# The beginning of a fused attention and two-layer MLP kernel: query transposes ahead of exponentials, row sums by ScalarE, three input weights prepared by GpSimd

## The chip, the cores and the metric

The kernel runs on 1 core of one Trainium2 chip. The metric is the device time of one execution in microseconds; three executions of the kernel before gave 1700.34, 1700.97 and 1705.41 us, a median of 1700.97 us.

## What is computed

Attention over keys and values that are averaged in groups of 8 rows, and then two MLPs of 4608 tokens, 512 to 2048 to 512, the first with a squared relu, the second with a leaky relu:

```python
k_p = k.reshape(B, H, Sp, 8, D).mean(axis=3)         # B = H = 8, D = 64, S = 576, Sp = 72
v_p = v.reshape(B, H, Sp, 8, D).mean(axis=3)
scores = scale * np.matmul(q, k_p.transpose(0, 1, 3, 2))
attn = np.exp(scores - np.max(scores, axis=-1, keepdims=True))
attn = attn / (np.sum(attn, axis=-1, keepdims=True) + 1e-09)
x = np.matmul(attn, v_p)                              # then to [4608, 512]
h = np.maximum(x @ w_in, 0.0);  x = h * h @ w_out     # moe_w_in, moe_w_out
h = x @ w2_in;  out = np.maximum(0.01 * h, h) @ w2_out
```

The weights arrive as 64-bit floats, and the kernel reads them as pairs of 32-bit words.

## The kernel before

**Tiling.** Tokens go in blocks of 512 (four tiles of 128). Matrix products are made in a split form: each operand is a high and a low part, and three products are added. One unit of the first product is 12 matmuls of 128x512 (`first`, L883). The kernel starts with the attention of block 0 alone (`start`), then makes 32 units of first products (`first_products`) of blocks 0 and 1, into which the attention of block 1 and the preparation of the weights are woven. After that everything is interleaved, and TensorE has work throughout.

**Order.** The program is recorded by hand: each engine runs its instructions in the order in which the code writes them. `START` is a list of words that `start()` (L749 on) works off: `K` and `Q` load keys and queries, `V` values and `i` a weight; `k0` pools, masks and transposes the keys of batch 0; `q` transposes a query tile and copies it out of PSUM with ScalarE (L567); `s` makes scores (L598), their negated maxima (VectorE, L610) and the exponentials (ScalarE, L619); `n` normalizes a tile (L630 to L640: row sums, reciprocal, product, and two copies of a remainder into one of two `prem` slots); `P` transposes the normalized tile and its remainder with TensorE (L661, L667) and copies the high part out with ScalarE (L671, L673); `r` makes the low part with VectorE (L680) and so gives the PSUM banks back; `v0` pools the values with TensorE (L392) and sums halves with VectorE (L402); `m0` splits the pooled values (L526 to L541); `w0` places them with ScalarE (L524); `x1` pools the keys of batch 1 with TensorE (L392). Then `values` (L712 to L715) makes the attention's output, and the first unit follows.

**Weights.** A weight of layer 1 is one load of 1 MB and seven steps (`weight_steps`): `a` scales the top words (ScalarE, L231), `b` shifts and merges their bits (VectorE, L235, L238), `c` cuts out the exponent and scales the low words by it (L249, L252), `d` adds (L293), `D` rounds to the high part (ScalarE, L298), `e` subtracts for the low part (VectorE, L302). All are 128x1024. Input weight n (0 to 7) is first used by units 2n and 2n+1. Weight 0 is made in `START`, the others by `conversion(u)` beside unit u; `val`, the work buffer, has 2 copies.

**Buffers and queues.** `bank()` hands out 4 PSUM banks in turn; `acc_bank` names four others. Loads are issued by SP in program order; stores of the first product's output (`mid`, L1098) are issued by GpSimd, which before the change does nothing else in the program but three memsets. The rows of `r`, from which they store, have 3 copies.

Of the kernel before, what the change touches and what calls it, by code (L numbers as in the profile page):

```python
# [16 lines left out]
P = 128  # L17
# [26 lines left out]
def attention_relu2_leaky_kernel(  # L44
# [27 lines left out]


# [3 lines left out]
        "K0 Q0 i0 Q1 Q2 Q3 V0 i1 K1 i2 Q4 Q5 i3 "  # L77
        "q0 k0 a0 s0 q1 b0 s1 q2 c0 n0 s2 q3 n1 s3 P0 d0 n2 r0 P1 n3 r1 a1 v0 P2 r2 m0 P3 r3 w0 e0 x1"
# [168 lines left out]
    def low_term(val, top, low):  # L247
# [4 lines left out]
        nc.vector.scalar_tensor_tensor(  # L252
            out=f32(low),
            in0=low,
            scalar=2.0**-52,
            in1=f32(top),
            op0=ALU.mult,
            op1=ALU.mult,
        )
# [13 lines left out]
    def weight_steps(w, kind, i):  # L273


        st = {}

# [10 lines left out]
        def term():  # L288
            low_term(st["val"], st["top"], st["low"])
# [14 lines left out]
        return load_words, lambda: exponent(st["top"]), bits, term, high, low, high_copy  # L304
# [77 lines left out]
    first_tiles, first_s, early = range(T // P), [], range(2 * T // P)  # L382
# [93 lines left out]
    def v_pool_pe(b):  # L476
# [3 lines left out]
        ps, last = acc_bank(2), acc_bank(3)  # L480
# [4 lines left out]
        halves_sum(vps[b], ps, 0, NP)  # L485
        halves_sum(vrps[b][:RROWS], last, 0, 2)
# [88 lines left out]
    def score_products(i):  # L575
# [12 lines left out]
        for hf in range(2):  # L588
            if i in first_tiles:
                ps = acc_bank((2 * i + hf) % KC)  # L590
            else:
                ps = acc_bank(KC - 1) if i in early and hf == 0 else bank()
# [145 lines left out]
    def start():  # L738

        t0, rest = 0, {}  # L740
        for word in START:
# [18 lines left out]
            elif x in "abcde":  # L760
                w1.do("dD" if x == "d" else x, n)
# [9 lines left out]
            elif x == "v":  # L771
                v_pool_pe(n)
                drop("v", n, NP)
                drop("rem", n, 2)
            elif x == "m":
# [282 lines left out]
    def conversion(u):  # L1058
        if u in begins:
# [595 lines left out]
```

## Time and profile before

| | |
|---|---|
| three runs | 1700.34, 1700.97, 1705.41 us |
| the profiled execution | 1704.66 us, of it the span 1702.9 us |
| busy: TensorE matmul, weight load | 1663.1 us (98%), 1500.0 us (88%) |
| busy: VectorE, ScalarE, GpSimd | 1156.0 us (68%), 703.9 us (41%), 19.6 us (1%) |
| first matmul of the first unit | 44.75 us from the span's start |

The span is the time between the first and the last recorded instruction; 1.8 us of the execution lie around it. In the rows below, PE is TensorE, DVE VectorE, ACT ScalarE, POOL GpSimd and SP the engine that issues loads. L12 is line 12 of the kernel before; in the kernel after, the functions that are named here stand 10 to 29 lines lower.

### The profile page before, as it was taken

How to read it: one execution, taken by the hardware profiler on the slowest of the kernel's cores; microseconds unless marked ns; L12 is line 12 of the kernel's file. 1: busy time of each engine (PE TensorE's matmuls, PEld its weight loads, DVE VectorE, ACT ScalarE, POOL GpSimd, SP SyncE). 2: the span in 40 equal slices, each digit the busy share in tenths (PEclk: the TensorE clock that was granted, in tenths of full speed). 3: DMA queues.
4: the chain of work that ended last, by engine and by line, in shares of the span. 5: the costliest groups of instructions: out<-in, count | busy, mean ns of one | idle time of the engine just before them, and what ended most of it. 6: DMA issues, size and time to landing. Idle time of an engine off the chain costs nothing. (4 is left out here: it accounts for less than half of the span.)

```text
span 1702.9 us, 25369 instructions
## 1 busy us (share of the span) xinstructions
PE 1663.1 (98%) x9608; PEld 1500.0 (88%) x9608; DVE 1156.0 (68%) x2028; ACT 703.9 (41%) x1551; POOL 19.6 (1%) x39
## 2 busy tenths in 40 slices
PE   6999999999999999999999999999999999999998
PEld 5778888888888888888888899999999999999998
DVE  7978886666666667575534677756767866666665
ACT  4545343343443443433433444434444633333332
POOL 0012000000000000000000000000000000000000
PEclk9999999999999999999999999999999999999999
DMA  8924542323233232332001255355437755454443
GB/s 229 342 88 156 173 152 94 89 89 96 88 98 98 86 97 74 96 110 73 30 25 56 86 172 177 118 179 174 170 126 257 259 164 164 150 158 155 155 149 106
DMA packets 197211, 228.24 MB, mean 134 GB/s; under 512 B 49120, under 2 KB 157920, under 8 KB 197088
## 3 DMA queue, kind: packets, MB, share of 16 engines
q1 hardware_dynamic: 193952, 217.70, 39.8%
q0 software_dynamic: 2560, 8.39, 1.3%
q8 instruction: 75, 1.23, 0.3%
q10 hardware_dynamic: 576, 0.52, 0.1%
q14 instruction: 48, 0.39, 0.1%
HBM read 140.58 MB, written 85.98 MB: 133 GB/s over the span
## 5 line engine op out<-in xcount | busy, mean ns | idle before, releaser
L883 PE MATMUL ps<-xh,wi 128*128 128x512 f32 x896 | 296.6, 393 | 0.0
L921 PE MATMUL acc<-gh,wo 128*128 128x512 f32 x1080 | 276.6, 394 | 0.7 <-ACT xl L893 0.7
L921 PEld LDWEIGHTS acc<-gh,wo 128*128 128x128 f32 x1080 | 200.7, 189 | 41.7 <-ACT xl L893 1.2
L883 PEld LDWEIGHTS ps<-xh,wi 128*128 128x128 f32 x896 | 168.2, 188 | 34.6 <-issue 0.2
L883 PE MATMUL ps<-xl,wi 128*128 128x512 f32 x448 | 174.4, 389 | 0.0
L900 DVE CAST gh<-r 128x512 fp32r<-128x512 f32 x112 | 47.6, 425 | 175.0 <-ACT r L896 174.6
L893 ACT ACTIVATE r<-ps 128x512 f32<-128x512 f32 x112 | 67.7, 605 | 207.8 <-PE ps L883 203.6
L921 PE MATMUL acc<-gl,wo 128*128 128x512 f32 x540 | 149.5, 390 | 0.0
L921 PEld LDWEIGHTS acc<-gl,wo 128*128 128x128 f32 x540 | 101.8, 189 | 21.6
L619 ACT ACTIVATE s<-ps,m 128x72 f32<-128x72 f32 x240 | 72.1, 330 | 93.4 <-DVE m L610 93.4
L883 PEld LDWEIGHTS ps<-xl,wi 128*128 128x128 f32 x448 | 84.2, 188 | 16.5
L1537 PE MATMUL acc<-wi,hh 128*128 128x256 f32 x512 | 94.0, 283 | 1.1 <-ACT r L1353 1.1
L1537 PE MATMUL acc<-wo,hh 128*128 128x256 f32 x512 | 93.8, 283 | 0.0
L1537 PE MATMUL ps<-wo,hh 128*128 128x256 f32 x496 | 90.9, 283 | 0.0
L1537 PE MATMUL ps<-wi,hh 128*128 128x256 f32 x496 | 90.9, 283 | 0.0
L1337 PE MATMUL acc<-fh,wi 128*128 128x384 f32 x408 | 88.4, 339 | 1.3 <-DVE gh L1350 0.3
L1337 PE MATMUL ps<-fh,wo 128*128 128x384 f32 x408 | 87.7, 337 | 0.0
L901 DVE TENSOR_TENSOR gl<-r,gh 128x512 fp32r<-128x512 f32 x112 | 77.6, 693 | 7.5
L1537 PEld LDWEIGHTS acc<-wi,hh 128*128 128x128 f32 x512 | 79.9, 192 | 1.3 <-ACT r L1353 1.3
L1537 PEld LDWEIGHTS acc<-wo,hh 128*128 128x128 f32 x512 | 79.9, 192 | 0.0
L1353 ACT ACTIVATE gh<-gh 128x384 f32<-128x384 f32 x48 | 25.3, 526 | 131.1 <-DVE gh L1350 131.1
L1537 PEld LDWEIGHTS ps<-wo,hh 128*128 128x128 f32 x496 | 77.4, 192 | 0.0
(278 smaller groups left out, 3560.9 us busy)
## 6 DMA issues: line engine op xcount, KB each, us to landing
hf<-r SPq DMA_DIRECT2D x96, 192.0 KB
xl<-hf SPq DMA_DIRECT2D x24, 640.0 KB
hr<-hf SPq DMA_DIRECT2D x24, 640.0 KB
xh<-hf SPq DMA_DIRECT2D x23, 640.0 KB
hf<-gl SPq DMA_DIRECT2D x48, 192.0 KB
hf<-gh SPq DMA_DIRECT2D x48, 192.0 KB
hf<-st SPq DMA_DIRECT2D x48, 192.0 KB
wi<-in_moe_w_in SPq DMA_DIRECT2D x8, 1024.0 KB
```

Source lines behind the costliest of these rows:

```text
L619: nc.scalar.activation(out=s[:, g, :], in_=ps[:, h * SP : (h + 1) * SP], func=AF.Exp, bias=m[:, g : g + 1], accum_out=None if i in early e ...
L883: nc.tensor.matmul(ps, lhsT=w[:, kc], rhs=x[kc], start=(kc == 0 and n == 0), stop=(kc == KC - 1 and n == 2),)
L893: nc.scalar.activation(out=r, in_=ps, func=AF.Relu)
L900: nc.vector.tensor_copy(gh, r)
L901: nc.vector.tensor_tensor(out=gl, in0=r, in1=f32(gh), op=ALU.subtract)
L921: nc.tensor.matmul(acc[m], lhsT=w[:, m * P : (m + 1) * P], rhs=x, start=(c == 0 and n == 0), stop=(c == FC - 1 and n == 2),)
L1337: nc.tensor.matmul(at, lhsT=w[:, FORMS[j], kc], rhs=x[j][:, kc], start=m == 0 and j not in (4, 6), stop=m == 5, skip_group_check=True,)
L1353: nc.scalar.activation(out=out_, in_=x, func=AF.Lrelu)
L1537: nc.tensor.matmul(at[:, s * TR : (s + 1) * TR], lhsT=x[:, a, s * P : (s + 1) * P], rhs=w[:, b], start=p == 0 and s == 0 and m == 0, stop= ...
```

## The change

It reorders `START`, lets GpSimd do steps `a`, half of `c`, `d` and `e` of input weights 0, 1 and 3, lets ScalarE's exponentials add up the rows of the first eight tiles, and moves steps of weights 1 to 3 between the beginning and the units.

```diff
+    BY_GPSIMD = (0, 1, 3)
     START = (
-        "K0 Q0 i0 Q1 Q2 Q3 V0 i1 K1 i2 Q4 Q5 i3 "
-        "q0 k0 a0 s0 q1 b0 s1 q2 c0 n0 s2 q3 n1 s3 P0 d0 n2 r0 P1 n3 r1 a1 v0 P2 r2 m0 P3 r3 w0 e0 x1"
+        "K0 Q0 Q1 Q2 i0 Q3 V0 i1 K1 i2 Q4 Q5 i3 "
+        "q0 k0 q1 s0 q2 s1 n0 q3 s2 a0 b0 c0 d0 n1 P0 s3 v0 r0 n2 P1 D0 a1 e0 "
+        "n3 u0 P2 m0 b1 c1 d1 r1 P3 w0 r2 x1 r3"
     ).split()
...
+    def exponent(top, engine=None):
+        if engine is None:
+            nc.scalar.activation(out=f32(top), in_=f32(top), func=AF.Copy, scale=2.0**-112)
+        else:
+            engine.tensor_scalar(out=f32(top), in0=f32(top), scalar1=2.0**-112, scalar2=None, op0=ALU.mult)
...
+    def low_term(val, top, low, engine=None):
+        engine = engine or nc.vector
         nc.vector.tensor_scalar(
             out=top, in0=val, scalar1=0xFF800000, scalar2=None, op0=ALU.bitwise_and
         )
+        if engine is nc.vector:
...
+        else:
+            engine.tensor_scalar(out=f32(low), in0=low, scalar1=2.0**-52, scalar2=None, op0=ALU.mult)
+            engine.tensor_tensor(out=f32(low), in0=f32(low), in1=f32(top), op=ALU.mult)
...
+        by = nc.gpsimd if kind == 0 and i in BY_GPSIMD else None
+        engine = by or nc.vector
...
-            nc.vector.tensor_tensor(out=w, in0=w, in1=f32(st["low"]), op=ALU.add)
+            engine.tensor_tensor(out=w, in0=w, in1=f32(st["low"]), op=ALU.add)
...
-            nc.vector.tensor_tensor(out=t[:, 1], in0=st["w"], in1=f32(t[:, 0]), op=ALU.subtract)
+            engine.tensor_tensor(out=t[:, 1], in0=st["w"], in1=f32(t[:, 0]), op=ALU.subtract)
...
-    first_tiles, first_s, early = range(T // P), [], range(2 * T // P)
+    first_tiles, first_s, early = range(T // P), [], range(0)
...
-        ps, last = acc_bank(2), acc_bank(3)
+        ps, last = bank(), bank()
         for cc in range(NP):
             halves(ps, cc, raws[("v", b, cc)][0], P)
         for c in range(2):
             halves(last, c, raws[("rem", b, c)][0], RROWS)
-        halves_sum(vps[b], ps, 0, NP)
-        halves_sum(vrps[b][:RROWS], last, 0, 2)
+        def rest():
+            halves_sum(vps[b], ps, 0, NP)
+            halves_sum(vrps[b][:RROWS], last, 0, 2)
+        return rest
...
     def conversion(u):
-        if u in begins:
+        if u == 0:
+            w1.do("De", 1)
+            w1.do("abcd", 2)
+        elif u == 1:
+            w1.do("D", 2)
+            w1.do("ab", 3)
+        elif u == 2:
+            w1.do("e", 2)
+            w1.do("c", 3)
+        elif u == 3:
+            w1.do("d", 3)
+        elif u == 4:
+            w1.do("De", 3)
+            w1.do("a", 4)
+        elif u in begins:
```

With `early` empty, the exponentials of tiles 0 to 7 get an accumulator output and the row sums of L630 are gone. The word `v` now only makes the products; `u` makes the two sums; `d` no longer includes `D`.

**TensorE, from tile 3's scores to the values**, where `acc_382<-gh` (before) and `acc_385<-gh` (after) begin `x1`. Before, from the second `P`:

```order
L661 MATMUL ps<-cst,wo_160 128x128 x4
L667 MATMUL ps<-cst,prem_82 96x128 x2
L392 MATMUL acc_314<-wo_99,cst 128x128 x12
L392 MATMUL acc_314<-wo_104,cst 128x128 x4
L392 MATMUL acc_315<-wo_104,cst 96x128 x8
L661 MATMUL ps<-cst,wo_160 128x128 x4
L667 MATMUL ps<-cst,prem_81 96x128 x2
L661 MATMUL ps<-cst,wo_250 128x128 x4
L667 MATMUL ps<-cst,prem_82 96x128 x2
L392 MATMUL acc_382<-gh,cst 128x128 x4
```

After, from the pooling of the values:

```order
L402 MATMUL ps<-wo_99,cst 128x128 x12
L402 MATMUL ps<-wo_104,cst 128x128 x4
L402 MATMUL ps<-wo_104,cst 96x128 x8
L675 MATMUL ps<-cst,wo_165 128x128 x4
L681 MATMUL ps<-cst,prem_82 96x128 x2
L675 MATMUL ps<-cst,wo_165 128x128 x4
L681 MATMUL ps<-cst,prem_81 96x128 x2
L675 MATMUL ps<-cst,wo_264 128x128 x4
L681 MATMUL ps<-cst,prem_82 96x128 x2
L402 MATMUL acc_385<-gh,cst 128x128 x4
```

The pooling of the values moved from behind `P1` to ahead of it and out of the named banks into two of the four that `P` uses in turn; `P1`, `P2`, `P3` and `x1` now follow each other.

**VectorE at the same place.** Before, from the copies of tile 3's remainder:

```order
L640 COPY prem_82<-wo_250 128x96 x2
L680 TENSOR_TENSOR ptl<-ps,pth 128x4x128
L680 TENSOR_TENSOR ptr<-ps,ptr 32x2x128
L402 TENSOR_REDUCE vp<-acc_314 128x256
L402 TENSOR_REDUCE vr<-acc_315 96x128
```

After, from the sums of the pooled values, which follow the same copies:

```order
L412 TENSOR_REDUCE vr<-ps 96x128
L540 TENSOR_SCALAR vh<-vp 128x256
L550 SCALAR_TENSOR_TENSOR vp<-vp,vh 128x256
L540 TENSOR_SCALAR rh<-vr 96x128
L550 SCALAR_TENSOR_TENSOR vr<-vr,rh 96x128
L540 TENSOR_SCALAR vr<-vr,cst 96x128
L555 SCALAR_TENSOR_TENSOR vr<-rh,cst,vr 96x128
L239 TENSOR_SCALAR val<-wi_112 128x1024
L242 SCALAR_TENSOR_TENSOR val<-wi_112,val 128x1024
L253 TENSOR_SCALAR wi_112<-val 128x1024
L694 TENSOR_TENSOR ptl<-ps,pth 128x4x128
```

`r1` (the last row) stood right behind the copies; now the value sums, `m0` and the bit steps of weight 1 (`wi_112`) stand ahead of it.

**GpSimd**, which had no instruction between the memset of `v_rem` and the first store of `mid`. After:

```order
L235 TENSOR_SCALAR wi_97<-wi_97 128x1024
L266 TENSOR_SCALAR wi_97<-wi_97 128x1024
L267 TENSOR_TENSOR wi_97<-wi_97 128x1024
L303 TENSOR_TENSOR val<-val,wi_97 128x1024
L235 TENSOR_SCALAR wi_112<-wi_112 128x1024
L312 TENSOR_TENSOR wi_245<-val,wi_245 128x1024
L266 TENSOR_SCALAR wi_112<-wi_112 128x1024
L267 TENSOR_TENSOR wi_112<-wi_112 128x1024
L303 TENSOR_TENSOR val<-val,wi_112 128x1024
L312 TENSOR_TENSOR wi_363<-val,wi_363 128x1024
L1127 DMA mid<-r 128x512
```

Weight 0 (`wi_97`, `wi_245`) and weight 1 (`wi_112`, `wi_363`) take five instructions each, and `a` of weight 1 stands ahead of `e` of weight 0.

## Rows read from the trace of the kernel before

**Rows 1.** The page's first part: busy us, share of the span, instructions.

```profile
PE 1663.1 (98%) x9608; PEld 1500.0 (88%) x9608; DVE 1156.0 (68%) x2028; ACT 703.9 (41%) x1551; POOL 19.6 (1%) x39
```

**Rows 2.** Windows: length, busy us of each engine, granted clock, DMA share, GB/s.

```profile
0.00:44.70 44.70, 28.33 (x181) 25.37 (x182) 32.57 (x64) 21.84 (x59) 0.73 (x5) 0.96 0.84 233
44.70:110.00 65.30, 57.89 (x305) 46.48 (x305) 55.72 (x96) 33.36 (x81) 6.53 (x11) 0.97 0.70 252
25.00:30.00 5.00, 4.66 (x26) 4.62 (x27) 3.90 (x10) 3.65 (x12) 0.00 (x0) 0.66 1.04 272
```

**Rows 3.** Timeline of PE, 29 to 45: start, us, engine, line, operation.

```profile
29.40 5.49 PE L392 MATMUL acc<-wo,cst 128*128 128x128 f32 x48
...
35.56 0.62 PE L661 MATMUL ps<-cst,wo 128*128 128x128 f32 x4
...
36.24 1.06 PE L392 MATMUL acc<-gh,cst 128*128 128x128 f32 x8
...
40.92 0.50 PE L712 MATMUL ps<-pth,v_hi 128*128 128x512 f32 x1
...
44.75 0.40 PE L883 MATMUL acc<-xh,wi 128*128 128x512 f32 x1
```

**Rows 4.** Timeline of DVE, 34 to 51.

```profile
34.28 0.41 DVE L640 COPY prem<-wo 128x96 f32<-128x96 f32 x2
34.72 0.69 DVE L680 TENSOR_TENSOR ptl<-ps,pth 128x512 fp32r<-128x512 f32 x1
...
35.90 0.69 DVE L402 TENSOR_REDUCE vp<-acc 128x256 f32<-128x512 f32 x1
...
36.95 0.69 DVE L680 TENSOR_TENSOR ptl<-ps,pth 128x512 fp32r<-128x512 f32 x1
...
38.12 0.29 DVE L526 TENSOR_SCALAR vh<-vp 128x256 fp32r<-128x256 f32 x1
...
40.06 0.69 DVE L680 TENSOR_TENSOR ptl<-ps,pth 128x512 fp32r<-128x512 f32 x1
...
47.77 0.68 DVE L235 TENSOR_SCALAR val<-wi 128x1024 uint32<-128x1024 uint32 x1
...
50.48 1.23 DVE L252 SCALAR_TENSOR_TENSOR wi<-wi 128x1024 f32<-128x1024 uint32 x1
```

**Rows 5.** Timeline of SP's issues and of ACT: two landings.

```profile
28.11 5.67 SPq L197 DMA_DIRECT2D raw<-in_q  x3
...
31.17 1.16 ACT L231 ACTIVATE wi<-wi 128x1024 f32<-128x1024 f32 x1 [0.20 <-DMA wi<-in_moe_w_in]
```

**Rows 6.** Waits of PE, 44.7 to 110: us in total, times, longest.

```profile
PE acc L883 <- DVE wi L302: 2.2, 4, 1.0
```

**Rows 7.** Timelines of POOL's issues and of DVE beside them, 54 to 88.

```profile
54.85 0.54 POOL L1098 DMA_DIRECT2D mid<-r  x1 [3.23 <-ACT r L893]
...
73.73 0.76 POOL L1098 DMA_DIRECT2D mid<-r  x1 [9.53 <-ACT r L893]
...
86.68 0.77 POOL L1098 DMA_DIRECT2D mid<-r  x1 [11.19 <-ACT r L893]
...
54.74 1.22 DVE L302 TENSOR_TENSOR wi<-val,wi 128x1024 fp32r<-128x1024 f32 x1
...
73.69 0.68 DVE L235 TENSOR_SCALAR val<-wi 128x1024 uint32<-128x1024 uint32 x1
...
86.66 0.68 DVE L235 TENSOR_SCALAR val<-wi 128x1024 uint32<-128x1024 uint32 x1
```

**Rows 8.** Timeline of POOL, its first microseconds.

```profile
0.73 0.52 POOL L1612 MEMSET v_rem<- 128x512 f32 x1 [0.29 <-POOLq L1634]
```

**Rows 9.** Line L630, duration in ns min/median/max, first and last start.

```profile
L630 DVE TENSOR_REDUCE l<-wo x4: 742/746/752, 20.2 to 32.2; 128x8 f32<-128x576 f32 x4
```

**Rows 10.** Line L619, the same columns.

```profile
L619 ACT ACTIVATION_READ_ACCUMULATOR s<-ps,m x224: 191/213/243, 182.3 to 868.9; 128x1 f32 x112
```

More of the change, by code (lines that the diff above doesn't have):

```diff
@@ L245, in first_bits @@
         )
-    def low_term(val, top, low):
+    def low_term(val, top, low, engine=None):
+        engine = engine or nc.vector
         nc.vector.tensor_scalar(
@@ L251, in low_term @@
         )
[L252 to L259, printed above, removed]
+        if engine is nc.vector:
+            engine.scalar_tensor_tensor(
+                out=f32(low),
+                in0=low,
+                scalar=2.0**-52,
+                in1=f32(top),
+                op0=ALU.mult,
+                op1=ALU.mult,
+            )
+        else:
+            engine.tensor_scalar(out=f32(low), in0=low, scalar1=2.0**-52, scalar2=None, op0=ALU.mult)
+            engine.tensor_tensor(out=f32(low), in0=f32(low), in1=f32(top), op=ALU.mult)
     def place(kind, i, t):
@@ L288, in term @@
         def term():
-            low_term(st["val"], st["top"], st["low"])
+            low_term(st["val"], st["top"], st["low"], by)
         def high():
             w = st["w"] = f32(st["val"])
-            nc.vector.tensor_tensor(out=w, in0=w, in1=f32(st["low"]), op=ALU.add)
+            engine.tensor_tensor(out=w, in0=w, in1=f32(st["low"]), op=ALU.add)
             t = st["parts"] = sb([P, 2, 1024], F32R, weight_tag(kind, i))
@@ L301, in low @@
             t = st["parts"]
-            nc.vector.tensor_tensor(out=t[:, 1], in0=st["w"], in1=f32(t[:, 0]), op=ALU.subtract)
-        return load_words, lambda: exponent(st["top"]), bits, term, high, low, high_copy
+            engine.tensor_tensor(out=t[:, 1], in0=st["w"], in1=f32(t[:, 0]), op=ALU.subtract)
+        return load_words, lambda: exponent(st["top"], by), bits, term, high, low, high_copy
     class Weights:
@@ L591, in score_products @@
             else:
-                ps = acc_bank(KC - 1) if i in early and hf == 0 else bank()
+                ps = acc_bank(KC - 1) if i < 2 * T // P and hf == 0 else bank()
             for b, _, r0, n in reversed(parts_of(i)):
@@ L759, in start @@
                 w1.load(n)
-            elif x in "abcde":
-                w1.do("dD" if x == "d" else x, n)
+            elif x in "abcdeD":
+                w1.do(x, n)
             elif x == "k":
@@ L771, in start @@
             elif x == "v":
-                v_pool_pe(n)
+                sums = v_pool_pe(n)
                 drop("v", n, NP)
                 drop("rem", n, 2)
+            elif x == "u":
+                sums()
             elif x == "m":
@@ L1062, in conversion @@
                 w1.do("a", n + 1)
-            w1.do("bcd" if n == 1 else "cdD", n)
+            if n > 3:
+                w1.do("cdD", n)
         elif u - 1 in begins:
             n = begins[u - 1]
-            if n == 1:
-                w1.do("D", n)
             if n < LAST and n + 1 != LATE:
                 w1.do("b", n + 1)
-            if n != LATE - 1:
+            if n not in (3, LATE - 1):
                 w1.do("e", n)
```

2 lines of the change are left out of this document (removed).

## The prediction

> **What bounds the kernel now.** I read the page's first part, then windows of the first 110 us, then the timelines of TensorE and VectorE there. TensorE's matmuls fill 98% of the span [rows 1], so a gain or a loss must come from the places where it has nothing to do. Two of them lie in the changed part: up to the first unit it is busy 28.33 of 44.70 us, and in the next 65.30 us it is busy 57.89 us [rows 2], which leaves 7.4 us. VectorE is busy 32.57 and 55.72 us there. The forecast is therefore about two things: when the first unit starts (44.75, [rows 3]), and what the 7.4 us become.
>
> What ends the beginning is read from the timeline of TensorE [rows 3]. From 29.40 it works nearly without a gap: the pooling of the values (5.49 us), then `P2`, `P3` (from 35.56), `x1` (from 36.24), the values (from 40.92) and the first unit. From `x1` to the values are 40.92 - 36.24 = 4.68 us, and from the values to the unit 3.83 us. What VectorE does meanwhile (`r1`, sums, `r2`, `m0`, `r3`, [rows 4]) runs beside `x1`. The two landings that count are fixed by the loads: SP's issue at 28.11 had waited for a load of the values, the last of the remainder, and weight 1 lands at about 31.1, where ScalarE waited for it [rows 5].
>
> **Part 1: the order of the beginning, with GpSimd's work at no cost.** The loads of tiles 1 and 2 go ahead of weight 0. Its landing moves back by two loads of 256 KB, about 2 us at the 233 GB/s of this stretch [rows 2]; nobody waits for it, since its bits now come behind the maxima of tile 2. Nothing is moved ahead of the remainder of the values or of weight 1 that was not ahead of them before, so both land as before.
>
> Now the pooling of the values stands ahead of `P1`, and TensorE can't pass 28.11. The last of its six groups of matmuls takes 5.49 / 6 = 0.9 us, so `P1` starts at 29.0 and, by the 0.68 us from `P3` to `x1` [rows 3], ends at 29.7. VectorE's copies of tile 3's remainder need the slot that `P1` reads: they start at 29.7. From there VectorE decides, by [rows 4]: copies 0.44 (34.28 to 34.72), sums 1.05 (35.90 to 36.95), `m0` 1.94 (38.12 to 40.06), the bits of weight 1 with the cut 2.71 (47.77 to 50.48), then `r1` 1.18 (34.72 to 35.90), which ends at 29.7 + 7.3 = 37.0. `P3` takes the two PSUM banks that `r1` gives back (four in turn: `P1` and `P3` share a pair), so it ends at 37.3; `x1` follows, and the values start at 37.3 + 4.68 = 42.0. Before it was 40.92: **+1.1 us**.
>
> So the 0.75 us row sums [rows 9] of four tiles, and three operations of 1.22 to 1.23 us of weight 0 [rows 4, 7], 6.7 us of VectorE in all, leave the beginning and give nothing: VectorE waits for TensorE at 29.7 whatever it saved ahead of that, and behind it 2.71 us were added in front of `r1`. The accumulator reads on ScalarE, 213 ns each [rows 10] and partly under the next exponential, lie ahead of 29 too: nothing.
>
> **Part 2: what a GpSimd operation costs.** No row shows GpSimd computing. The nearest is its memset of 128x512 in 0.52 us [rows 8]. At that rate 128x1024 takes 1.05 us, the lower end; two operands and a result that each take such a pass give 3.1 us, the upper end. I take 1.05 us for one operand and 2.1 us for two, since the memset is nearest and the reads come on top. The Trainium skill, GPSIMD Engine Reference, section Elementwise — side-by-side cycle accounting, has 4497 ns for an addition of 2048 columns, by which I estimate 2.25 us here: 0.15 us more for each such operation. No row tells.
>
> If these ran freely, they would be in time: weight 0's chain is ready at about 35 for a unit that starts at 46.
>
> **Part 3: what they cost VectorE.** GpSimd's store issues show it. Most take 0.54 us. At 73.73 and at 86.68 they took 0.76 and 0.77, and beside them ran a shift of VectorE, 128x1024 in 0.68 us from SBUF to SBUF (73.69 to 74.37, 86.66 to 87.34): each issue ended 0.12 and 0.11 us after the shift did [rows 7]. A fast one-operand operation of VectorE holds GpSimd up until it is done. I take it that the reverse holds too, for the length of a GpSimd operation. At 54.85 an issue ran beside a two-operand operation (54.74 to 55.96) in 0.54 us, not held up; but it reads no tile. So for VectorE's two-operand operations the wait is between nothing and the whole; I take nothing, the row's value.
>
> The order of GpSimd then places three operations in a row behind weight 1's landing: `a` of weight 1, `e` of weight 0, the scaling of weight 1's low words: 1.05 + 2.1 + 1.05 = 4.2 us, from 31.2 to 35.4. VectorE is then at `m0`, whose first operation starts at 29.7 + 0.44 + 1.05 = 31.2; a fast operation of it is held until 35.4, or some 3.7 us, and `r1`, `P3`, `x1` and the values come behind it: **+3.7 us**. At 1.05 us for all GpSimd operations it is 2.6, at 3.1 for two operands 4.7. Waits ahead of 28 (copies behind weight 0's products, about 1 us) vanish in the wait for the remainder.
>
> **Part 4: the units.** TensorE's waits for low parts of weights [rows 6] shrink by the one of weight 1, the longest, 1.0 us. Against that ScalarE now rounds weight 1 ahead of the copy of tile 4's queries (about 1.05 us, of which 0.9 reach TensorE), and VectorE's shift of weight 2 waits for `e` of weight 1 on GpSimd, which starts about 0.9 us earlier: 1.2 us. Sum **+1.1 us**; the copies of tiles 4 and 5 may add as much. VectorE is lightened here by the four row sums and some ten operations, but the remaining waits are for chains through ScalarE and the transposes. The stores wait behind GpSimd's work; `r` has 3 copies, which covers one operation of 2 us.
>
> **Part 5: the clock.** From 25 to 30 the granted clock was 0.66 on average [rows 2], a part at 1.2 instead of 2.4 GHz, after TensorE had mostly waited. After the change it waits longer, from about 31 to 40, and then `x1` decides. A stretch at half rate of the same length, 5.00 x 0.34 x 2 = 3.4 us, would cost 1.7 there; before it cost about 0.9. **+0.8 us**, between -0.9 and +2.
>
> **Sum.** 1.1 + 3.7 + 1.1 + 0.8 = +6.7 us against the profiled execution's 1704.66, 1711.4. That execution is 3.7 us above the median 1700.97, and I move the sum to the median: **1707.7 us**.
>
> **Rivals.** *Nothing is held up* (the forecast on the other side: not slower). GpSimd reads beside VectorE freely; for it speaks the issue at 54.85. Parts 1, 4 without the hold and 5 remain: 1.1 - 1.0 + 0.9 + 0.8 = +1.8, 1702.8 us, within 0.3% of before, about what a measurement can tell from no change (5.1 us). It decides as soon as the fast operations of `m0` show their durations of before, back to back.
>
> *Both kinds of VectorE operations are held.* Then tile 1's normalization waits for two operations of weight 0 (about 4 us, of which 1.4 vanish in the wait for the remainder) and tile 4's for two of weight 3: some +2.9 more, 1710.6 us; at 3.1 us a product about 1715. The Trainium skill, SBUF — State Buffer, section SBUF: two separate sides, says that VectorE operations in a two-port mode or with two SBUF inputs and GpSimd operations that read SBUF exclude each other for a whole instruction. By that rule this rival is the forecast; the trace agrees for the fast operations, at 73.73 and 86.68, and no row here shows the other kind.
>
> *VectorE's relief reaches the end* (faster): if the beginning is set by VectorE's total, not by TensorE's wait at 28.11, it saves 6.7 - 2.71 = 4.0 us, and of the units' waits for weights, 2.2 us [rows 6], perhaps 1.7: 1695.3 us. Against it: `r1` stands behind more work than before, and `x1` behind `r1`.
>
> **Chances.** Fast operations held, as summed: 0.38, from +4 to +9, a quarter of it under 5.1. Both kinds held: 0.23. Nothing held: 0.28. Relief: 0.11, most of it past -0.3%. So slower by over 0.3%: 0.29 + 0.23 = 0.52; within 0.3%: 0.09 + 0.28 + 0.01 = 0.38; faster by over 0.3%: 0.10. The range leaves out the relief, under 1698, and the dear end of the second rival, over 1715; inside it are both ends of GpSimd's price and of the clock. Slower and not slower are both open; the likeliest case's own range is 1705 to 1710.
>
> **What would show it.** Right: `P1` waits until 28 to 29; a fast VectorE operation of `m0` is late by 3 to 4 us while GpSimd runs three operations from about 31.2; the first unit starts at 49 to 51; GpSimd's two-operand operations take 2 to 2.3 us. Wrong: the first unit at or before 45, VectorE operations back to back beside GpSimd's, or GpSimd operations that are far from 1 to 3 us. The forecast fails to the fast side if the hold falls where VectorE would wait anyway, and to the slow side if the products are held up too.

## The result, and the profile after

The changed kernel takes 1716.25 us (median of 4 runs, 1715.94 to 1718.54), the kernel before 1703.05 us (4 runs, 1700.34 to 1705.41). The ratio is 1.0075, 95% interval 1.0062 to 1.0087: **slower by 13 us**. The forecast was 1707.7 us with a range from 1698 to 1715.0: the sign is right, the size is half, and the range is missed by 1.25 us. The profiled execution took 1716.16 us, its span 1714.4 us; against that of before the span is 11.5 us longer.

The page's first part answers to [rows 1]:

```profile
PE 1664.6 (97%) x9608; PEld 1500.9 (88%) x9608; DVE 1150.7 (67%) x2011; ACT 705.4 (41%) x1612; POOL 58.7 (3%) x54
```

TensorE's busy time is 1.5 us more than before, VectorE's 5.3 less, GpSimd's 39 more: VectorE got the relief that the change gives it, and 10 of the 11.5 us are idle time of TensorE. Where it lies, the timeline of TensorE shows (start, us, engine, line, operation; the bracket is the idle time before it and who ended it; answers to [rows 3]):

```profile
28.45 0.60 PE L675 MATMUL ps<-cst,wo 128*128 128x128 f32 x4
...
31.34 0.63 PE L675 MATMUL ps<-cst,wo 128*128 128x128 f32 x4 [2.06 <-DVE vp L412]
...
40.74 1.08 PE L675 MATMUL ps<-cst,wo 128*128 128x128 f32 x4 [8.56 <-DVE ptl L694]
...
42.05 1.91 PE L402 MATMUL acc<-gh,cst 128*128 128x128 f32 x8
...
47.79 0.50 PE L726 MATMUL ps<-pth,v_hi 128*128 128x512 f32 x1
...
51.62 0.40 PE L899 MATMUL acc<-xh,wi 128*128 128x512 f32 x1
...
71.94 1.33 PE L612 MATMUL acc<-kt,qt 128*128 128x144 f32 x4 [3.25 <-ACT qt L581]
```

`P1` is at 28.45, `P2` at 31.34, `P3` at 40.74, `x1` at 42.05, the values at 47.79, the first unit at **51.62 instead of 44.75: +6.9 us**. From there to the end of the span are 1714.4 - 51.62 = 1662.8 us, before 1702.9 - 44.75 = 1658.15: **+4.6 us**. TensorE's waits from 28 to 125 us (total, times, longest) name the two places:

```profile
PE ps L675 <- DVE ptl L694: 8.6, 1, 8.6
PE acc L612 <- ACT qt L581: 4.8, 4, 3.2
PE ps L675 <- DVE vp L412: 2.1, 1, 2.1
```

The 8.6 us are `P3`, which waits for the PSUM banks that `r1` gives back; the 3.2 us are tile 5's scores, which wait for the copy of its queries. The granted clock is at 1.2 instead of 2.4 GHz from 34, within the first wait, to 44.3, and again behind the second; a third such stretch, at 116 to 119.5, lies in the values of block 1, behind a wait of 1.4 us (windows: length, busy us of each engine, clock, DMA share, GB/s):

```profile
34.00:45.00 11.00, 4.26 (x23) 4.27 (x24) 9.17 (x10) 3.04 (x8) 9.65 (x4) 0.53 0.46 136
71.00:75.00 4.00, 3.06 (x13) 3.06 (x14) 2.86 (x9) 1.39 (x3) 3.92 (x3) 0.57 1.04 412
116.00:120.00 4.00, 4.00 (x14) 3.52 (x13) 1.88 (x3) 1.60 (x4) 0.00 (x0) 0.58 0.17 66
```

Before, two stretches had such a clock: one at 26 to 29.4 us, behind the last wait of the beginning, and one at 104.3 to 107.6, in the values of block 1 too. So the long stretch up to 44.3, in place of the one at 26, and the one at 71 are what the change brought. A stretch of some 3.4 us at half rate costs 1.7 us where TensorE is the bound, so a difference of less than that between two single profiles is not read as an effect in what follows.

What VectorE did while `P3` waited, and what it did ahead of tile 4's maxima (its timeline; [rows 4] has the durations of before):

```profile
22.62 2.31 DVE L647 TENSOR_TENSOR wo<-wo,l 128x576 f32<-128x576 f32 x1
...
31.44 0.61 DVE L540 TENSOR_SCALAR vh<-vp 128x256 fp32r<-128x256 f32 x1
...
32.99 0.76 DVE L540 TENSOR_SCALAR vr<-vr,cst 96x128 f32<-96x128 f32 x1
33.79 2.33 DVE L555 SCALAR_TENSOR_TENSOR vr<-rh,cst,vr 96x128 f32<-96x128 f32 x1
36.05 0.68 DVE L239 TENSOR_SCALAR val<-wi 128x1024 uint32<-128x1024 uint32 x1
36.76 1.99 DVE L242 SCALAR_TENSOR_TENSOR val<-wi,val 128x1024 uint32<-128x1024 uint32 x1
38.78 1.22 DVE L253 TENSOR_SCALAR wi<-val 128x1024 uint32<-128x1024 uint32 x1
39.92 0.67 DVE L694 TENSOR_TENSOR ptl<-ps,pth 128x512 fp32r<-128x512 f32 x1
...
58.03 1.90 DVE L239 TENSOR_SCALAR val<-wi 128x1024 uint32<-128x1024 uint32 x1 [3.31 <-issue]
59.97 2.34 DVE L242 SCALAR_TENSOR_TENSOR val<-wi,val 128x1024 uint32<-128x1024 uint32 x1
...
67.86 0.45 DVE L624 TENSOR_REDUCE m<-acc 128x4 f32<-128x288 f32 x1
```

and GpSimd beside it:

```profile
22.43 1.89 POOL L267 TENSOR_TENSOR wi<-wi 128x1024 f32<-128x1024 f32 x1 [0.84 <-DVE l L645]
...
30.79 2.88 POOL L235 TENSOR_SCALAR wi<-wi 128x1024 f32<-128x1024 f32 x1 [3.62 <-DMA wi<-in_moe_w_in]
33.64 2.33 POOL L312 TENSOR_TENSOR wi<-val,wi 128x1024 fp32r<-128x1024 f32 x1
36.06 3.39 POOL L266 TENSOR_SCALAR wi<-wi 128x1024 f32<-128x1024 uint32 x1
...
56.99 2.39 POOL L312 TENSOR_TENSOR wi<-val,wi 128x1024 fp32r<-128x1024 f32 x1 [12.47 <-ACT wi L308]
```

GpSimd's products, sums and differences take 1.89 to 2.44 us, once 2.77 (weight 0's sum, beside tile 1's normalization); its scalings, with one operand, take 2.88 to 3.9. The last operation of `m0`, 0.35 us in every profile without GpSimd beside it, took 2.33: it started at 33.79 and ended 0.15 us after GpSimd's subtraction (33.64 to 35.97). The multiplication of tile 1's normalization (22.62) ended 0.6 us after GpSimd's product; alone it takes 0.76. Beside the scalings VectorE lost less: 0.33 us (at 31.44), 0.48, 0.76 and 0.53.

Tile 4's maxima start 16.2 us after the first unit (67.86), in the kernel before 11.1 us (its timeline of VectorE):

```profile
55.88 0.45 DVE L610 TENSOR_REDUCE m<-acc 128x4 f32<-128x288 f32 x1
```

GpSimd's holds are a part of that, the late start of VectorE's first word another: the bits of weight 2 start 6.4 us after the first unit (58.03), where the bits of weight 1 started 3.0 us after it before (47.77, [rows 4]). They need `a` of weight 2, which ScalarE does only behind the rounding of weight 1 (timeline of ScalarE, after):

```profile
56.80 1.14 ACT L233 ACTIVATE wi<-wi 128x1024 f32<-128x1024 f32 x1
```

### The profile page after: what moved, and what is told of

Same layout as the page of the kernel before. It is cut to its first block, busy times and chain, and to the rows that moved or that the text cites. A ratio compares the mean times of both kernels' runs of the same rounds, so it can differ in the third digit from the quotient of the medians.

```text
span 1714.4 us, 25438 instructions
## 1 busy us (share of the span) xinstructions
PE 1664.6 (97%) x9608; PEld 1500.9 (88%) x9608; DVE 1150.7 (67%) x2011; ACT 705.4 (41%) x1612; POOL 58.7 (3%) x54
## 3 DMA queue, kind: packets, MB, share of 16 engines
q8 instruction: 75, 1.23, 0.3%
## 5 line engine op out<-in xcount | busy, mean ns | idle before, releaser
L937 PEld LDWEIGHTS acc<-gh,wo 128*128 128x128 f32 x1080 | 200.7, 189 | 41.9 <-ACT xl L909 1.2
L1382 ACT ACTIVATE gh<-gh 128x384 f32<-128x384 f32 x48 | 25.3, 526 | 130.5 <-DVE gh L1379 130.5
```

The costliest lines, as they stand in the source:

```text
L937: nc.tensor.matmul(acc[m], lhsT=w[:, m * P : (m + 1) * P], rhs=x, start=(c == 0 and n == 0), stop=(c == FC - 1 and n == 2),)
L1382: nc.scalar.activation(out=out_, in_=x, func=AF.Lrelu)
```

## The experiments

All ratios are against the kernel before on the same chip. "First unit" is its first matmul in the profile, "rest" the span behind it, as a difference to the 1658.15 us of before. Both are of one profiled execution, the ratio is of all.

| run | ratio (95% interval) | first unit | rest |
|---|---|---|---|
| after | 1.0075 (1.0062 to 1.0087) | 51.62 | +4.6 |
| e1 no GpSimd | 1.0102 (1.0068 to 1.0136) | 56.76 | +6.8 |
| e2 GpSimd alone | 1.0073 (1.0049 to 1.0096) | 49.38 | +7.4 |
| e3 row sums alone | 1.0003 (0.9984 to 1.0023) | 46.57 | -1.2 |
| e5 train by ScalarE | 1.0054 (1.0039 to 1.0070) | 48.28 | +2.8 |
| e6 r1 ahead | 1.0056 (1.0043 to 1.0070) | 48.55 | +4.2 |
| e7 weight 3 later | 1.0069 (1.0055 to 1.0082) | 52.65 | +3.3 |
| e8 weight 0 alone | 1.0019 (1.0010 to 1.0028) | 41.95 | +3.8 |
| e9 weight 3 off | 1.0073 (1.0058 to 1.0089) | 52.86 | +3.9 |
| e10 new order, no GpSimd | 0.9979 (0.9970 to 0.9988) | 42.10 | -1.2 |
| e11 the same, weight 0 by GpSimd | 0.9980 (0.9971 to 0.9989) | 43.34 | -0.9 |
| e12 sums 4 to 7 back | 1.0079 (1.0062 to 1.0095) | 53.08 | +5.3 |
| e13 e9 with sums 4 to 7 back | 1.0060 (1.0045 to 1.0075) | 53.49 | +2.1 |
| e14 e10 with all sums | 0.9987 (0.9978 to 0.9997) | 41.50 | -0.6 |
| e15 e8 with sums 4 to 7 back | 1.0015 (1.0003 to 1.0027) | 42.72 | +1.3 |

**The three parts apart.** The first three runs take the change to pieces. e1 is the kernel after with an empty list:

```diff
-    BY_GPSIMD = (0, 1, 3)
+    BY_GPSIMD = ()
```

> The kernel after, with the list of GpSimd's weights empty: its operations go back to VectorE and ScalarE, the new order and the row sums by ScalarE stay. Theory (the order costs little, the GpSimd train costs most): VectorE's fast operations of m0 take 0.21 to 0.29 us each and its last one (two operands, 96x128) 0.35 us instead of 2.33; in front of r1 now stand 1.23 + 1.22 us more of VectorE's own work on weight 1, so r1 ends at about 39.4 instead of 41.1 and the first unit starts at 48 to 49 instead of 51.6; the wait of 3.2 us for tile 5's queries shrinks below 1. Against the kernel before +3 to +6 us (1.002 to 1.0035). Rival (the order itself costs it, whoever does the work): first unit at 51 or later, +10 us or more (1.006).

The rival won, by more than it asked: 1.0102, first unit at 56.76. Its timeline of ScalarE shows why:

```profile
21.61 1.29 ACT L233 ACTIVATE wi<-wi 128x1024 f32<-128x1024 f32 x1
```

and its timeline of VectorE, what follows:

```profile
22.93 0.69 DVE L239 TENSOR_SCALAR val<-wi 128x1024 uint32<-128x1024 uint32 x1 [4.13 <-ACT wi L233]
...
29.61 0.81 DVE L624 TENSOR_REDUCE m<-acc 128x4 f32<-128x288 f32 x2
```

`a` of weight 0 now stands on ScalarE behind tile 2's exponentials and ends at 22.9; VectorE waits 4.1 us for it with its next word, and tile 3's maxima (25.3 in the kernel after) come at 29.61. So the order of the kernel after is bad by itself, and worse without GpSimd: with `a` of weight 0 at this place it needs a GpSimd that does it. e2 is the other half: the kernel before with `BY_GPSIMD = (0, 1, 3)` and the changed weight steps, nothing else.

> The kernel before, with GpSimd's steps of input weights 0, 1 and 3 alone: its order of the beginning, its conversions and its row sums by VectorE stay. Theory (GpSimd costs most): the beginning loses under 1 us, since nothing of GpSimd stands beside m0 there but the scaling of weight 1's top words and e of weight 0; in the units weight 1 comes late by 3 to 5 us (product 1.9, sum 2.4, subtraction 2.4 us instead of one of 1.23 each, behind each other) and weight 3 by 1 to 3: +4 to +8 us (1.0025 to 1.005). Rival (only the order costs): 0 to +2 us.

Between the two: GpSimd costs, but 13 us, not 4 to 8. I had given the beginning under 1 us; it lost 4.6. Its timeline of VectorE:

```profile
22.67 2.78 DVE L642 TENSOR_TENSOR wo<-wo,l 128x576 f32<-128x576 f32 x1
```

and its waits of TensorE from 28 to 125:

```profile
PE acc L607 <- ACT wo L576: 4.2, 1, 4.2
PE acc L892 <- ACT wi L307: 3.5, 2, 2.9
PE acc L892 <- POOL wi L311: 2.2, 1, 2.2
```

Tile 1's normalization is held 2.0 us by GpSimd's sum for weight 0 (and 1.2 by its product just before); tile 2's maxima stand behind it, its exponentials behind these, and behind them on ScalarE the copy of tile 3's queries, for which TensorE waits 4.2 us. In the units weight 1 comes late, as expected: 2.9 us for the high part, 2.2 for the low. e3 is the kernel before with the row sums by ScalarE alone:

```diff
-    first_tiles, first_s, early = range(T // P), [], range(2 * T // P)
+    first_tiles, first_s, early = range(T // P), [], range(0)
```

> The kernel before, with the row sums of the first eight tiles by ScalarE's accumulator alone. Theory: in the beginning nothing (the exponentials end ahead of the last load of the values); in the units each tile's eight exponentials take 0.7 us longer on ScalarE (0.295 us apart instead of 0.205) and VectorE 0.75 us less: -1 to +1.5 us (0.9995 to 1.001). Rival (ScalarE's exponentials stand on the path of the query copies): +2 to +4 us.

As expected: no effect that can be measured, though the interval would allow 4 us. The parts don't add up: 19 us (the new order with the sums) and 13 us (GpSimd) make 13 together.

**What a GpSimd operation costs and holds (e4).** A kernel of its own, with GpSimd's operations and VectorE's on scratch tiles of 128x1024, 3 and 8 of a kind that start together:

```diff
+        for own in (lambda: ts((top, top)), lambda: ts((b, a)), lambda: add(a, b, c)):
+            for rest in (fast, flat, two, from_psum):
...
+                for n in range(3):
+                    own()
+                for n in range(8):
+                    rest()
```

> No part of the reference is computed: tiles of zeros go out. GpSimd's operations run first with every other engine idle, then VectorE's alone, then GpSimd's and VectorE's in pairs that start together behind one ScalarE operation. Theory (GpSimd excludes VectorE from SBUF for whole operations, with both kinds of VectorE operations): GpSimd alone shows 2.9 us for one operand and 1.9 to 2.4 us for two at 128x1024 whether the words stand 4 or 8 bytes apart; beside GpSimd's two-operand operations VectorE's one-operand (0.69 us) and two-operand (1.23 us) ones wait up to 2.4 us, those from PSUM never; beside its one-operand operations they wait 0.3 to 1.1 us, not the whole 2.9. Rival (a one-operand operation of GpSimd takes 1.05 us alone and is 2.9 us in the kernel because VectorE held it up): 1.0 to 1.2 us alone.

VectorE's memsets and the VectorE-alone chains overlapped the start, so "alone" is read from GpSimd's operations beside VectorE's from PSUM. Duration in ns (minimum/median/maximum), first and last start; in turn VectorE's one-operand and two-operand operations beside GpSimd's one-operand ones, the same two beside its two-operand ones (the first five of the one-operand ones still ran beside a scaling, at most 1.40 us long), VectorE's from PSUM beside these, then GpSimd's one-operand beside PSUM work and beside VectorE's one-operand ones, its two-operand beside PSUM work and beside VectorE's two-operand ones:

```profile
L85 DVE TENSOR_SCALAR x<-go x8: 694/1074/1459, 35.0 to 42.4; 128x1024 uint32<-128x1024 uint32 x8
L95 DVE TENSOR_TENSOR db<-go,dc x8: 1224/1604/2015, 55.0 to 66.2; 128x1024 f32<-128x1024 f32 x8
L85 DVE TENSOR_SCALAR x<-go x8: 694/1400/2712, 116.5 to 125.7; 128x1024 uint32<-128x1024 uint32 x8
L95 DVE TENSOR_TENSOR db<-go,dc x8: 1224/1225/3246, 143.5 to 158.4; 128x1024 f32<-128x1024 f32 x8
L98 DVE TENSOR_TENSOR db<-go,ps x8: 686/687/689, 160.8 to 165.9; 128x512 f32<-128x512 f32 x8
L79 POOL TENSOR_SCALAR w<-w x3: 2884/2886/3313, 69.7 to 75.6; 128x1024 f32<-128x1024 f32 x3
L79 POOL TENSOR_SCALAR w<-w x3: 3282/3626/3745, 35.8 to 43.4; 128x1024 f32<-128x1024 f32 x3
L82 POOL TENSOR_TENSOR pa<-pb,pc x3: 2340/2349/2350, 161.3 to 166.2; 128x1024 f32<-128x1024 f32 x3
L82 POOL TENSOR_TENSOR pa<-pb,pc x3: 3201/3201/3202, 145.0 to 151.6; 128x1024 f32<-128x1024 f32 x3
```

One operand costs GpSimd 2.88 us at 8 bytes a word and 2.77 side by side (102 to 122 us), two operands 2.35: the scaling is the dear one, and 1.05 was far off. Beside two-operand work VectorE's operations wait up to 2.0 us (2.71 - 0.69, 3.25 - 1.23), both kinds, and GpSimd's wait for them too (3.20 instead of 2.35). Beside one-operand work they wait at most 0.8 (1.46 - 0.69, 2.02 - 1.22), several times, and GpSimd's operation grows to 3.75. From PSUM nothing is held (0.687 throughout).

**The beginning.** e5 takes the train of 30.8 to 39.5 us off GpSimd; the subtraction for weight 0's low part is left out, with a ScalarE copy in its place:

```diff
+            if by_act:
+                nc.scalar.activation(out=f32(low), in_=low, func=AF.Copy, scale=2.0**-52)
...
+            if by and i == 0:
+                nc.scalar.copy(t[:, 1], st["w"])
+                return
...
+        return load_words, lambda: exponent(st["top"], None if i == 1 else by), bits, term, high, low, high_copy
```

> The kernel after, with the three GpSimd operations of the train that starts at 30.8 us taken off GpSimd: ScalarE scales weight 1's top and low words, and the subtraction for the low part of weight 0 is left out, a ScalarE copy of the same shape stands in its place. Order and instructions of VectorE and TensorE are those of the kernel after. Theory (VectorE between the sums of the values and r1 is held for 3.75 us by this train: 0.48 + 1.98 + 0.76 + 0.53): those operations take 0.28, 0.35, 1.23 and 0.69 us, r1 ends at 37.3 instead of 41.1, the first unit starts at 47.5 to 48 instead of 51.6, and the time is 3 to 4 us under the kernel after: 1.005 to 1.0055 against before. Rival (the order alone puts r1 there, the hold falls into a wait): first unit at 51 to 52, 1.0075.

1.0054, 3.8 us under the kernel after: what the theory says, though the two intervals overlap a little. VectorE's timeline settles it: the operations are back at their lengths, and `r1` ends at 36.84 (in the kernel after at 41.05). The expected 3.75 us leave out the first operation of `m0`, 0.61 us beside the scaling and 0.28 here; with it the holds are 4.1 us.

```profile
32.86 0.35 DVE L561 SCALAR_TENSOR_TENSOR vr<-rh,cst,vr 96x128 f32<-96x128 f32 x1
...
33.84 1.23 DVE L242 SCALAR_TENSOR_TENSOR val<-wi,val 128x1024 uint32<-128x1024 uint32 x1
35.10 0.69 DVE L253 TENSOR_SCALAR wi<-val 128x1024 uint32<-128x1024 uint32 x1
...
36.42 0.42 DVE L700 TENSOR_TENSOR ptr<-ps,ptr 32x256 fp32r<-32x256 f32 x1
```

The first unit gains 3.3 us of the 4.2, since there `x1` runs at half clock up to about 41.9 and takes 6.6 us instead of 4.7. e6 moves one word:

```diff
-        "n3 u0 P2 m0 b1 c1 d1 r1 P3 w0 r2 x1 r3"
+        "n3 u0 P2 r1 m0 b1 c1 d1 P3 w0 r2 x1 r3"
```

> The kernel after, with r1 moved ahead of m0, b1, c1 and d1 in the order of the beginning, nothing else. Theory (r1 releases the PSUM banks of P3, and m0 and the bits of weight 1 in front of it cost TensorE its 8.6 us wait): r1 ends at 32.7, P3 starts at once, x1 from 33.5; now the last low part (r3) comes last, behind m0, b1, c1 with their holds, at 43.3, the values start there instead of at 47.8 and the first unit at 47.2 instead of 51.6: 4 to 4.5 us under the kernel after, 1.0045 to 1.0055 against before. Rival (whatever stands there, VectorE's sum up to the values decides): values at 47 or later, no gain.

1.0056: 3.2 us under the kernel after, less than the 4 to 4.5 expected. `P3` and `x1` are early, the values wait for `r3`, as worked out, but at 42.0; what was missed is the clock, at half rate behind that wait, so that the values take 6.5 us instead of 3.8 and the unit starts at 48.55 (timeline of TensorE):

```profile
33.26 1.06 PE L402 MATMUL acc<-gh,cst 128*128 128x128 f32 x8
...
42.02 0.77 PE L726 MATMUL ps<-pth,v_hi 128*128 128x512 f32 x1 [4.01 <-DVE ptl L694]
```

**The units.** e7 gives weight 3 its place of before (the conversions' table):

```diff
         elif u == 1:
             w1.do("D", 2)
-            w1.do("ab", 3)
         elif u == 2:
             w1.do("e", 2)
-            w1.do("c", 3)
+            w1.do("ab", 3)
         elif u == 3:
-            w1.do("d", 3)
+            w1.do("cd", 3)
```

> The kernel after, with a and b of weight 3 one unit later (beside unit 2) and its c with d beside unit 3. Theory (in unit 1 a of weight 3 on GpSimd holds VectorE's bits of weight 2 for 1.6 us, and b of weight 3 puts 1.9 us ahead of tile 4's maxima, so that its exponentials and, behind them, the copy of tile 5's queries are late): the wait of 3.2 us for that copy falls under 0.7 us, weight 3 costs up to 1 us more: 1.5 to 3 us under the kernel after. Rival (ScalarE's longer exponentials and its rounding of weights make the wait): it stays above 2 us and the time stays.

The named wait went as the theory has it, from 3.25 to 0.72, and the time hardly moved (1.0069). TensorE's timeline has the reason: the next query copy became the late one.

```profile
70.48 0.76 PE L612 MATMUL acc<-kt,qt 128*128 128x144 f32 x4 [0.72 <-ACT qt L581]
...
83.82 1.33 PE L612 MATMUL acc<-kt,qt 128*128 128x144 f32 x4 [2.17 <-ACT qt L581]
```

It stands on ScalarE behind weight 3's rounding, which waits for GpSimd's sum. e9 is e7 with `BY_GPSIMD = (0, 1)`.

> The kernel of the run with weight 3 later (a and b beside unit 2, c and d beside unit 3), and weight 3 given back to ScalarE and VectorE; weights 0 and 1 stay with GpSimd. Theory (GpSimd's chain for a weight, 2.9 + 1.9 + 2.4 + 2.4 us and its hold of VectorE, reaches TensorE through ScalarE's query copies, and each wait over 2 us brings a stretch at half clock behind it): no wait for a query copy over 1.2 us is left between 52 and 125 us, no halved clock from 55 to 100, and the time is 2 to 4 us under the run with weight 3 later: 1.0045 to 1.006 against before. Rival (the waits come from ScalarE's accumulators and the order of its queue): a wait of 2 us stays, no gain.

A miss: no gain (1.0073). A wait of 1.75 us for tile 5's copy is left, and a halved clock at 81 to 85. Two numbers of the same trace fit the 1.75 us, but no run takes the first away by itself: VectorE's shift for weight 2 takes 1.91 instead of 0.69 beside GpSimd's subtraction for weight 1, and the exponentials of tile 4 take 2.44 us on ScalarE (67.17 to 69.61) instead of 1.80 (56.36 to 58.16) before. e12 and e13 take the accumulators of block 1 away, from the kernel after and from e9:

```diff
-    first_tiles, first_s, early = range(T // P), [], range(0)
+    first_tiles, first_s, early = range(T // P), [], range(4, 8)
```

> The kernel after, with the row sums of tiles 4 to 7 back on VectorE; block 0 keeps ScalarE's accumulators. Theory (in the units ScalarE is the path from maxima to the next query copy, and the accumulators make it 8 x 0.09 = 0.7 us longer for each tile): the wait for tile 5's query copy falls from 3.2 to 2.5 us, the others by up to 0.7, and the time by 0.7 to 2 us: 1.006 to 1.007 against before. Rival (only GpSimd's holds and the order of the conversions make these waits): no change, or 0.75 us more for each tile's normalization.

> The kernel of the run with weight 3 off GpSimd, with the row sums of tiles 4 to 7 back on VectorE. Theory (its waits of 1.75 us for tile 5's copy and 1.35 us behind tile 5's exponentials come from the accumulators, 0.7 us each, and from the hold of weight 2's bits, 1.2 us): both waits fall by 0.6 to 0.7, the halved clock at 81 to 85 goes: 1.5 to 3 us under that run. Rival (the conversions' order): the same time.

In e12 the wait falls as said, 3.25 to 2.43, and the time doesn't: VectorE now has the sums beside GpSimd's weight 3, and tile 4's normalization is held to 2.29 us, tile 5's to 2.78. In e13 (1.0060) the wait is 1.0 and the time 2.0 us under e9, in the range expected, with intervals that overlap; the halved clock stayed. So in the units each removed wait uncovers the next.

**Together, and better than both.** e8 joins the edits: weight 0 alone on GpSimd, `r1` ahead, weight 1's bits behind `r3`, weight 3 later.

```diff
-    BY_GPSIMD = (0, 1, 3)
+    BY_GPSIMD = (0,)
...
-        "n3 u0 P2 m0 b1 c1 d1 r1 P3 w0 r2 x1 r3"
+        "n3 u0 P2 r1 m0 P3 w0 r2 x1 r3 b1 c1 d1"
```

> The kernel after with GpSimd for weight 0 alone, r1 ahead of m0, the bits of weight 1 behind r3, weight 3 later as in the run before: the three edits that the theory asks for, together. Theory: the beginning loses its wait for r1 and nearly all holds (only the subtraction of weight 0 stands beside m0, up to 2 us), first unit at 43 to 45.5, units as before, with 0.7 us longer exponentials: -2 to +2 us against the kernel before. Rival (the order of the beginning is worse by itself): +4 us or more.

The first unit starts at 41.95, earlier than expected, but its second matmul waits (timeline of TensorE):

```profile
43.97 0.50 PE L899 MATMUL acc<-xl,wi 128*128 128x512 f32 x1 [1.64 <-DVE xl L704]
```

VectorE makes that operand, the low part of the attention's output, behind weight 1's bits. The second unit starts at 48.35, in the kernel before at 48.90: the beginning gained 0.5 us, and a part of the rest of +3.8 belongs to it. The ratio of 1.0019 (3.0 us) lies a little over the theory's range, with nothing of GpSimd's arithmetic left in the units. So e10 and e11 take the conversions of before, and put the pooling of the values into banks that leave `P1` and `P2` alone:

```diff
-        "K0 Q0 i0 Q1 Q2 Q3 V0 i1 K1 i2 Q4 Q5 i3 "
-        "q0 k0 a0 s0 q1 b0 s1 q2 c0 n0 s2 q3 n1 s3 P0 d0 n2 r0 P1 n3 r1 a1 v0 P2 r2 m0 P3 r3 w0 e0 x1"
+        "K0 Q0 Q1 Q2 i0 Q3 V0 i1 K1 i2 Q4 Q5 i3 "
+        "q0 k0 q1 s0 q2 a0 s1 n0 q3 s2 b0 n1 P0 s3 c0 d0 v0 r0 n2 P1 D0 a1 "
+        "n3 P2 r1 P3 u0 r2 m0 w0 x1 r3 e0"
...
-        ps, last = acc_bank(2), acc_bank(3)
+        ps, last = acc_bank(0), acc_bank(1)
```

> No GpSimd at all: the kernel before with the loads of the kernel after, query transposes ahead, row sums of block 0 by ScalarE, the pooling of the values ahead of P1 but in the two accumulator banks that tile 2's scores leave (so the four banks in turn stay free for P1 and P2), the scaling of weight 0 on ScalarE ahead of tile 1's exponentials, and in the end P2, r1, P3, sums, r2, m0; the conversions of before. Theory (the reordering is worth something once nothing stands in front of r1 and nothing holds VectorE): first unit at 41.5 to 43 instead of 44.75, units as before: -1.5 to -3.5 us against before (0.998 to 0.999). Rival (the remainder's landing at 28 and the path behind it fix the beginning whatever the order): 0 to +2 us.

> The run without GpSimd, but weight 0 made by GpSimd as in the kernel after (its bits behind the maxima of tile 2, its low part behind P1). Theory (GpSimd's work ahead of 28 falls into the wait for the remainder; only the subtraction of weight 0, 2.4 us from about 31.5, can hold VectorE): first unit within 1 us of the run without GpSimd, time within 1.5 us of it. Rival (GpSimd's relief of VectorE, 6 us of weight 0's work, is what lets the order gain): 2 us or more faster than the run without GpSimd.

Both are **faster than both kernels**: 0.9979 and 0.9980 (1700.15 and 1701.31 us where before has 1704.16). With weight 0's work taken from VectorE it is no faster. In the timeline of TensorE of e10 `P3` waits 0.8 us, and nothing longer stands between it and the unit at 42.10:

```profile
32.06 0.63 PE L675 MATMUL ps<-cst,wo 128*128 128x128 f32 x4 [0.83 <-DVE ptl L694]
```

Last, e14 puts all row sums on ScalarE in e10, and e15 takes those of tiles 4 to 7 away in e8:

> The kernel of the run with the new order and no GpSimd, with the row sums of tiles 4 to 7 by ScalarE too. Theory (with the conversions of before ScalarE and VectorE have slack there, as the run with the sums alone showed): within 1.2 us of it. Rival (accumulators cost 0.7 us for each of four tiles wherever they stand): 2 to 3 us slower.

> The kernel of the run with GpSimd for weight 0 alone, with the row sums of tiles 4 to 7 back on VectorE; nothing of GpSimd is left beside the units but its store issues. Theory (the conversions of the kernel after, which put a to d of weight 2 ahead of tile 4's maxima, cost the units 2 to 3 us by themselves): first to fourteenth unit 71 to 72.5 us as without this edit (72.05) against 69.3 before, time within 1.5 us of that run. Rival (the accumulators cost the units these 2 to 3 us): 69 to 70 us, 2 us or more faster.

e14 is 0.9987, by the ratios 1.4 us over e10, where the theory allowed 1.2 and the rival asked for 2 to 3. The intervals overlap and the two spans are equal (1699.0 us), so under the conversions of before a cost of the accumulators is neither shown nor excluded. e15 (1.0015) stays within 1.1 us of e8, as the theory has it, in favour of the order of the conversions. The rests of the two, +1.3 and +3.8, are no measure for the accumulators: 1.6 us of the difference is e8's wait in its first unit, and the profiled execution of e15 was the fastest of its ten.

The pair that shows the cost of the conversions is e11 and e15. Both leave GpSimd weight 0 alone and the sums of tiles 4 to 7 to VectorE, and their second units start at 47.49 and 47.56. The ratios are 0.9980 and 1.0015, with intervals that don't meet: 6 us, where the two beginnings end alike and what differs behind them are the conversions. (The two profiled executions, e15's being its fastest, differ by 1.5 us behind the second unit.) In the table the rest is -1.2 to -0.6 in the four runs with the conversions of before and no GpSimd in the units, and +1.3 to +6.8 in all with those of after, whoever does the work; with GpSimd's weights 1 and 3 under the conversions of before (e2) it is +7.4. So the conversions of after and GpSimd's work in the units both cost; how the 4.6 us of the kernel after split between them stays open, since the parts cover each other and a single halved stretch is 1.7 us.

## Why the prediction was right in the sign and wrong in the size

The forecast lies 8.5 us under the result. 2.1 us of it is the base: 1700.97 was the median of three runs, with the fourth it is 1703.05, and 1703.5 to 1704.2 in the later groups. Another 1.7 us is the profiled execution of before, 1704.66, which the sum was made against: spans differ by 11.5, medians by 13.2. The other 4.8 us are the sum: 6.7 forecast, 11.5 found, 1.3 of the difference in the beginning and 3.5 behind the first unit, in part 4, the step that failed.

- **Part 1, order, +1.1: right.** `P1` was forecast at 29.0 and came at 28.45; `r1` was to end at 37.0 without a hold, and ends at 36.84 in e5. That relief of VectorE ahead of 28 gives nothing also held: e11, with that work on GpSimd, is no faster than e10.
- **Part 2, price: half wrong.** Two operands 2.1, measured 1.89 to 2.44 and once 2.77, under the bound of 3.1; one operand 1.05, measured 2.88 to 3.9. The memset, which reads nothing, was the wrong neighbour. The estimate of 2.25 us from the Trainium skill, GPSIMD Engine Reference, section Elementwise — side-by-side cycle accounting, agrees with the 2.35 us of e4 for two operands; for one operand it gave no figure here.
- **Part 3, hold, +3.7: the sum near, the step wrong.** From the start of `m0` to `r1` VectorE lost 0.33 + 0.48 + 1.98 + 0.76 + 0.53 = 4.1 us, and e5 shows that it is this train and that it reaches the end. (By the prediction's own times, an operation held from 31.2 to 35.4, the term would be 4.2; why it was put at 3.7 isn't said.) But I let one fast operation wait for the whole train, and two-operand ones not at all. The traces show that the largest piece, 1.98, is a two-operand operation behind GpSimd's subtraction, and that one-operand work of GpSimd held the others for 0.3 to 0.8 each. Two errors, a price too low and a hold too long, cancelled: that the sum is near is luck.
- **Part 4, units, +1.1: the step that failed.** Measured +4.6. TensorE's waits for weights fell by the 1.0 of the sum (2.8 us before, 1.8 after; the low parts alone from 2.2 [rows 6] to 0.5). The copy of tile 4's queries, priced at 0.9, made it wait 0.17. The hold of weight 2's shift by weight 1's subtraction was forecast as 1.2 and is 1.22. What I left out is the path to the copy of tile 5's queries, which is late by 3.25 us; for it I had only the remark that the copies may add as much again. On that path stand the late start of weight 2's bits, behind `a` on ScalarE; `a` of weight 3 on GpSimd, which holds the next two operations by 1.1 and 0.5; `b` of weight 3, 1.9 us ahead of tile 4's maxima; and 0.65 us of accumulators behind them, which I had priced only ahead of 28 us. The runs that take single ones away shorten the wait (e7 to 0.72, e12 to 2.43) and gain no time beyond the noise, so their shares stay open.
- **Part 5, clock, +0.8: too small.** The halved stretch of the beginning came as a mechanism, but from 34 to 44.3, so that `P3` and `x1` lost 1.7 us together (0.6 at `P3`, 1.1 from `x1` to the values), and a further one came at 71 behind the new wait. The 1.7 is what the part itself has for a halved stretch; the 0.9 that it takes off for the stretch of before was not gained, since part 1 already has TensorE wait up to 28.

**The rivals.** *Nothing held* fell: e5 gains 3.8 us by moving the train alone. *Both kinds held* is what the traces show for GpSimd's two-operand work, and with up to 1715 us it was the nearest; I gave it 0.23. The rule behind it (the Trainium skill, SBUF — State Buffer, section SBUF: two separate sides: the one that starts first keeps the ports for its whole instruction) agrees with e4 for GpSimd's sums, 2.0 us of waiting on either kind and none from PSUM; for its one-operand work the measured waits of at most 0.8 us out of 2.88 speak against a hold for the whole instruction. *Relief reaches the end* fell in e10 against e11, for the work on weight 0. That there were gains in the beginning at all is shown by e10, by its order together with block 0's row sums on ScalarE; the sums alone, in the order of before (e3), gave none.

## What to carry to other kernels

Before work is moved to an idle engine, ask what stands behind it in the order of the engine that is not idle: here the words in front of `r1`, which gives PSUM banks back, made TensorE wait 8.6 us, and moving `r1` ahead of them gained 3.2; in e10 another order, without GpSimd, brought the first unit 2.6 us ahead of before. GpSimd's elementwise work is priced by its own operation, not by a memset, and charged to VectorE as well: its two-operand work held VectorE's SBUF operations for up to 2.0 us in e4 and left those from PSUM alone, so it belongs beside PSUM work. And a mechanism that is found in one stage has to be charged in every stage where the same operations meet: the hold and the accumulators were priced in the beginning and, for the most part, forgotten in the units.

## What was not expected of the hardware

- GpSimd's multiplication by a constant, one operand, takes longer (2.88 us, 2.77 with words side by side) than its addition of two tiles (2.35 us) at 128x1024, with nothing in its way.
- The hold differs by GpSimd's operation: in e4 VectorE's 0.69 us operation takes up to 2.71 beside its additions of 2.67, and up to 1.46 beside its scalings of 2.88 and more, several times within one.
- A tiny operation is held as well: in e2 VectorE's addition on 128x8, 0.17 us, took 1.38 at 21.02 beside GpSimd's product, which ended at 22.37.
- The granted clock of TensorE fell to 1.2 GHz behind waits of 2.2 us (before, at 103; e7, at 84), 2.4 (e12), 3.25 (after, at 72) and 4.0 (e6). Within the wait of 8.6 us it was down from 34 on, and with TensorE busy 4.26 of 11 us it stayed there up to 44.3 (0.53 on average from 34 to 45). The length of a wait alone doesn't tell: in the kernel after it stayed at 2.4 GHz up to 34 behind the 2.06 us ahead of `P2`, and fell at 116 behind 1.4 us. By these numbers the wait of 3.25 us cost nearer 5, an estimate: 3.25 and up to 1.7 for the halved stretch.
